# Two more attention groups with an elementwise bonus, a new written order for the first tile, and three down projections in a row at the end

## The chip, the cores and the metric

The kernel runs on one core of a Trainium2 chip. The metric is the device time of one execution in microseconds (us). Three runs of the kernel before took 530.88, 531.82 and 531.77 us; the median is 531.77 us. The core has five engines that run their own instruction queues in order: TensorE (PE in the profile; its weight loads are listed as PEld), VectorE (DVE), ScalarE (ACT), GpSimd (POOL) and SyncE (SP), which here only issues DMAs.

## The reference

The program is a recurrent linear attention whose output goes through a gated feed-forward block.

- Attention, for 4 batches, 8 heads, 768 positions and head size 48: `y[t] = r[t] @ (state + (u*k[t]) v[t]^T)`, then `state = w * state + k[t] v[t]^T`. The term with `u` is the bonus: it weighs the position's own key and value.
- Feed-forward, for the 3072 rows of width 384 that the attention gives: `gate = sigmoid(x @ w_gate)`, `val = x @ w_val` (both 384 to 1536), `out = (gate * val) @ w_out` (1536 to 384). All in float32.

## The kernel before, in words

**Attention.** The 768 positions are cut into 12 chunks of 64, the heads into 2 sets, which gives 24 groups, numbered n = 0 to 23 (`GROUPS`, line 34; chunk n // 2). A group's work is: scores of keys against queries (`scores`, 64 small matmuls on TensorE or 32, see below), a masked copy of the scores into `score` (`keep`, VectorE), outputs from the state of the chunk before (`from_state`, 32 small matmuls, none for chunk 0), outputs from the scores (`apply`, 32), the chunk's contribution to the state (`outer`, 32), the decay of the state (ScalarE) and its sum (VectorE). `x_high` (ScalarE) and `x_low` (VectorE) split the outputs into two float32r parts in `xt`, the input of the feed-forward. `fills` moves rows of `xt` inside SBUF with DMAs.

**The bonus, in two ways** (`FIRST`, line 39). Groups below `FIRST` get it from TensorE: ScalarE scales the keys by u (`bonus_keys`, four instructions), `scores` makes a second set of 32 matmuls of these against the queries, and `keep` copies its diagonal with a second masked copy. `apply` puts a drain of TensorE between the outputs from the state and those from the scores, since the two use the array's quarters differently. Groups from `FIRST` on get it elementwise: the queries in token order are loaded into `dec` (`load_own`), GpSimd multiplies them by the keys and by u (`own_tokens`, two instructions), VectorE sums over the head size and spreads the sums over a diagonal (`diagonal`, two instructions), and ScalarE turns a part of the queries round (`turn_queries`, two copies). The state is laid out differently from `FIRST` on; the two groups before it change it over (`add_state`, lines 435 to 453).

**Feed-forward.** The rows are cut into 6 tiles of 512 columns (two chunks each), the 1536 hidden columns into 12 blocks f. An item is one block of one tile: `up` (18 matmuls of 512 columns, 9 for the gate and 9 for the value, each half into its own bank of a ring of three PSUM banks), `gate` (sigmoid on ScalarE, product on VectorE, `h_high` on ScalarE, `h_low` on GpSimd) and `down` (9 matmuls into three accumulators). `h` has two buffers (pool `hq`). A matmul is split in three float32r products (`PASS`). In the first tile the first two blocks are done in halves of 256 columns, one per chunk, which makes items 0 to 3; items 4 to 13 are blocks 2 to 11 of the first tile.

**Weights.** Each of the 12 blocks (1152 KB) is loaded as 64-bit floats and turned into two float32r parts on the core: `cast_top` (ScalarE), `join_words` (VectorE), `round_weights` (ScalarE), `rest_of_weights` (GpSimd or VectorE).

**Order.** The engines follow the written order (`manual_schedule`); a wait stops all that stands behind it on its engine. `START` (lines 43 to 57) is the order of groups 0 to 7 and items 0 to 13, one step a word: L, X, Y, W load channels (512 KB), tokens (400 KB), own tokens (192 KB) and weights; A are the bonus keys, R/Rv the queries (GpSimd/VectorE), t their turn, k the keys, T/Tv the token keys; Z `scores`, K `keep`, I `apply` with the outputs from the state, O `outer`, d and s (sa on ScalarE) decay and sum of the state, h and l the two parts of x, F `fills`; b and i `own_tokens` and `diagonal`; c, j, w and o/ov the four steps of a block of weights (c0, j0, w0, o0 for halves of block 0); U `up`, g, m, H and q/qv the four steps of the gate (qv: `h_low` on VectorE), D `down`; tc, tk, ti, tp, tr, tt, tn make constants and decay tables. All loads go through SP's queue in this order. Channels and tokens have three buffers each, `dec` two, the ring of banks three: a load waits at the head of SP's queue for a free buffer.

From item 14 on a loop (line 674) writes the order: for each item `up`, at four of twelve items one attention group (from n = 8), `gate`, and then `down` of the item before. After the last item `store_last` scales the accumulators on ScalarE and VectorE in turn and issues four DMAs on SP.

Of the kernel before, what the change touches and what calls it, by code (L numbers as in the profile page):

```python
# [35 lines left out]
TILE_OF = [c // 2 for c in range(NC)]  # L36


HALF, FIRST = 2, 8
SLOTS = (0, 3, 6, 9)  # L40


START = """
L.0 W.0 L.1 X.0 W.1 L.2 X.1 X.2 tc A.0 tk ti.1 R.0 ti.0 k.0 tp tr Z.0 tt K.0 I.0 c0.0 A.1 c0.1 tn
h.0 c.1 T.2 T.1 k.1 Rv.1 j0.1 l.0 Tv.0 j0.0 Z.1 O.0 W.2 F.0 W.3 L.3 L.4 W.4 X.3 j.1 K.1 I.1 O.1 A.2
w0.0 sa.0 w.1 h.1 w0.1 o0.1 o.1 R.3 Rv.2 k.2 o0v.0 l.1 s.1 Z.2 K.2 U.0 I.2 O.2 g.0 c.2 d.2 A.3 m.0
U.1 H.0 g.1 h.2 j.2 k.3 s.2 l.2 q.0 T.3 m.1 F.2 L.5 W.8 X.4 L.6 W.5 W.6 L.7 X.5 F.1 X.6 L.8 W.7 Z.3
K.3 I.3 O.3 w.2 A.4 k.4 H.1 c.3 h.3 l.3 R.4 D.0 Z.4 U.2 d.3 s.3 g.2 c.4 j.3 w.3 j.4 qv.1 m.2 o.2
U.4 H.2 g.4 w.4 A.5 K.4 q.2 U.3 D.2 g.3 Rv.5 m.3 k.5 ov.3 m.4 T.4 I.4 O.4 Z.5 H.3 A.6 d.4 h.4 H.4
c.6 c.5 k.6 s.4 K.5 l.4 Tv.5 j.6 R.6 q.3 D.1 D.3 U.5 I.5 g.5 h.5 j.5 qv.4 l.5 m.5 o.4 Z.6 D.4 R.7  # L50
O.5 U.6 A.7 d.5 H.5 K.6 k.7 s.5 q.5 T.6 w.5 ov.5 U.7 c.8 c.7 g.6 j.7 m.6 L.9 X.8 ub Y.8 W.9 W.10
X.7 I.6 Z.7 O.6 D.5 w.6 g.7 ov.6 d.6 w.7 H.6 s.6 j.8 qv.6 h.6 l.6 m.7 w.8 ov.7 H.7 qv.7 D.6 U.8 K.7
R.8 c.9 ov.8 g.8 m.8 Tv.7 H.8 U.9 qv.8 g.9 k.8 j.9 w.9 o.9 m.9 D.7 U.10 g.10 H.9 c.10 j.10 m.10 q.9
D.8 I.7 H.10 d.7 Z.8 O.7 h.7 w.10 D.9 s.7 U.11 ov.10 l.7 W.11 F.5 X.9 F.6 F.3 F.7 F.4 Y.9 qv.10
g.11 c.11 j.11 D.10 U.12 m.11 w.11 R.9 ov.11 U.13 g.12 H.11 qv.11 m.12 H.12 qv.12 g.13 t.8 D.11 b.8
i.8 D.12 K.8 k.9 m.13 H.13 q.13 b.9 T.9 t.9 i.9 T.8
"""


# [1 line left out]
def rwkv_then_moe(ctx: ExitStack, tc: tile.TileContext, wd, ub, ch, tk, rt, wt, rk0, vn0, wd0, out):  # L61
    nc = tc.nc
# [33 lines left out]
    w = wu[:, 0]  # L96
# [292 lines left out]
    def apply(n):  # L389
        c, g = GROUPS[n]  # L390
        v, t = toks[n][:, 1], score[n % 2]
        if n < FIRST:
            outputs(n)
            if c:
                nc.tensor.drain()
        for p, p2 in PP:
            for s in range(2):
                for gm in range(2):
                    be, row = gm ^ s, slice(64 * gm, 64 * gm + 64)
                    m, at = D if s else 64, (4 * p + 2 * be + p2) * D  # L400
# [101 lines left out]
    class Moe:  # L502
# [34 lines left out]
            c, h = self.cols, self.h[f]  # L537
            eng.tensor_tensor(h[:, 1, c], self.sg.pop(f)[:, c], h[:, 0, c], ALU.subtract)  # L538

        def gate(self, f):  # L540
            self.sigmoid(f)
            self.product(f)
            self.h_high(f)
            self.h_low(f)

        def down(self, f):

# [63 lines left out]
    def finish(i):  # L611
        ti, h, f = items[i]
        moe_of(items[i]).down(f)
        if f == NF - 1:
            if ti == len(TILES) - 1:
                store_last(accs[ti], TILES[ti][0])
            else:
                store(accs[ti], slice(TILES[ti][0], TILES[ti][-1] + 1))
# [274 lines left out]
```

## Time and profile before

| | |
|---|---|
| runs of the kernel before | 530.88, 531.82, 531.77 us; median 531.77 us |
| profiled execution | 534.72 us, of which the span from first to last instruction is 532.9 us |
| TensorE busy | 510.4 us, 96% of the span |
| VectorE, ScalarE, GpSimd busy | 203.4, 186.9, 189.9 us |
| DMA from memory and back | 47.84 MB, on SP's queue |

The profile is of one execution, slower than the median of the others. Busy TensorE time is modelled: a matmul's bar lasts longer than the distance to the next, so the distance between weight loads (PEld) says more about the pace than the bars do. A line of the timeline merges instructions of one kind: start, time from the first start to the last end, engine, source line, operation, names and shapes, count, and in brackets the idle time before it and what ended that.

### The profile page before, as it was taken

The numbers are of one execution on the slowest core, as the hardware profiler recorded it, in microseconds if no ns is written. First come the engines' busy times: TensorE is split into PE (matmuls) and PEld (weight loads), VectorE is DVE, ScalarE is ACT, GpSimd is POOL, SyncE is SP. The second block draws the span as 40 slices with busy tenths as digits, with TensorE's granted clock in tenths as the row PEclk, the third lists the DMA queues.
The fourth block names the chain that finished last, engine by engine and source line by source line (L and its number), as shares of the span: only waits on it lengthen the run. The fifth ranks groups of instructions, "written<-read, shape, count | busy, mean of one in ns | idle before, by whom it ended". The sixth has DMA issues, their size and how long they took to land. (4 is left out here: it accounts for less than half of the span.)

```text
span 532.9 us, 11951 instructions
## 1 busy us (share of the span) xinstructions
PE 510.4 (96%) x5204; PEld 424.4 (80%) x5204; DVE 203.4 (38%) x344; ACT 186.9 (35%) x396; POOL 189.9 (36%) x159
## 2 busy tenths in 40 slices
PE   3689999999999999999999999999999999999994
PEld 3678878888888888888888888888888888888883
DVE  8857868464243242341431532431442211111111
ACT  5577665545133233233232331331432222212111
POOL 4362530406453352443452552542253111112210
PEclk9999999999999999999999999999999999999999
DMA  8939736030321230420221420312400000100001
GB/s 321 366 111 352 301 112 284 4 103 21 127 87 26 71 106 1 145 86 17 80 61 48 145 87 0 97 34 72 146 17 2 11 11 10 60 0 1 0 2 64
DMA packets 15723, 47.84 MB, mean 90 GB/s; under 512 B 2384, under 2 KB 5200, under 8 KB 14256
## 3 DMA queue, kind: packets, MB, share of 16 engines
q1 hardware_dynamic: 15664, 47.01, 25.3%
q8 instruction: 43, 0.70, 0.6%
q14 instruction: 16, 0.13, 0.1%
HBM read 39.92 MB, written 4.72 MB: 84 GB/s over the span
## 5 line engine op out<-in xcount | busy, mean ns | idle before, releaser
L516 PE MATMUL ring<-xt,wx 128*128 128x512 f32 (+1 forms) x1332 | 309.9, 387 | 0.9 <-ACT sg L525 0.5
L516 PEld LDWEIGHTS ring<-xt,wx 128*128 128x128 f32 x1332 | 247.8, 191 | 51.3 <-ACT sg L525 0.7
L538 POOL TENSOR_TENSOR h<-sg,h 128x512 fp32r<-128x512 f32 (+1 forms) x66 | 88.5, 1340 | 259.5 <-ACT h L534 259.5
L554 PE MATMUL acc<-h,wx 128*128 128x512 f32 (+1 forms) x666 | 161.6, 388 | 0.4 <-POOLq L714 0.4
L554 PEld LDWEIGHTS acc<-h,wx 128*128 128x128 f32 x666 | 121.2, 188 | 25.6 <-POOLq L714 0.8
L529 DVE TENSOR_TENSOR sg<-ring,sg 128x512 f32<-128x512 f32 (+1 forms) x74 | 50.0, 676 | 237.0 <-PE ring L516 235.6
L525 ACT ACTIVATE sg<-ring 128x512 f32<-128x512 f32 (+1 forms) x74 | 43.4, 586 | 157.4 <-PE ring L516 157.4
L534 ACT CAST h<-sg 128x512 fp32r<-128x512 f32 (+1 forms) x74 | 45.0, 608 | 144.2 <-DVE sg L529 138.2
L293 POOL TENSOR_TENSOR dec<-chan,tabk 128x512 f32<-128x512 f32 x21 | 29.0, 1381 | 12.5 <-PE ring L337 12.4
L478 DVE TENSOR_TENSOR xt<-ring,xt 112x256 fp32r<-112x256 f32 (+1 forms) x52 | 19.9, 418 | 33.1 <-ACT xt L474 33.0
L308 POOL TENSOR_TENSOR toks<-toks,tabn 128x384 f32<-128x384 f32 x19 | 24.0, 1267 | 13.7 <-DMA toks<-in_tk 13.7
L314 POOL TENSOR_TENSOR dec<-dec,toks 128x384 f32<-128x384 f32 x16 | 16.3, 1020 | 27.3 <-DMA dec<-in_rt 27.3
L304 DVE TENSOR_TENSOR chan<-chan,tabk 128x512 f32<-128x512 f32 x24 | 25.0, 1042 | 0.9 <-ACT dec L287 0.9
L375 PE MATMUL sc<-dec,chan 48*64 48x64 f32 x768 | 17.4, 231 | 7.7 <-DVE chan L304 7.6
L383 DVE COPY_PREDICATED score<-masks,sc 128x512 f32<-128x512 int32 x32 | 23.9, 747 | 1.9 <-PE sc L375 1.1
L428 ACT ACTIVATE state<-state,pw 112x96 f32<-112x96 f32 x80 | 23.4, 362 | 2.6 <-PE ring L337 2.6
L337 PE MATMUL ring<-score,toks 64*48 64x64 f32 (+1 forms) x768 | 17.2, 230 | 5.0 <-DVE score L383 4.1
L447 DVE TENSOR_TENSOR state<-state,ring 48x192 f32<-48x192 f32 (+1 forms) x52 | 17.9, 350 | 9.7 <-ACT xt L474 4.7
L375 PEld LDWEIGHTS sc<-dec,chan 48*64 48x64 f32 x768 | 15.0, 145 | 8.1 <-POOL dec L293 7.6
L247 DVE SCALAR_TENSOR_TENSOR wf<-wr,top 128x1152 int32<-128x1152 int32 (+1 forms) x13 | 16.9, 1310 | 9.4 <-ACT top L240 5.7
L337 PEld LDWEIGHTS ring<-score,toks 64*48 64x48 f32 (+1 forms) x768 | 14.6, 137 | 6.4 <-DVE score L383 4.8
L474 ACT CAST xt<-ring 112x256 fp32r<-112x256 f32 (+1 forms) x52 | 16.7, 364 | 7.6 <-PE ring L337 7.3
(60 smaller groups left out, 250.5 us busy)
## 6 DMA issues: line engine op xcount, KB each, us to landing
wr<-in_wt SPq DMA_DIRECT2D x11, 1152.0 KB, 9.2
chan<-in_ch SPq DMA_DIRECT2D x24, 512.0 KB, 4.2
toks<-in_tk SPq DMA_DIRECT2D x24, 400.0 KB, 4.8
out_y<-wf SPq DMA_DIRECT2D x17, 256.0 KB, 2.5
dec<-in_rt SPq DMA_DIRECT2D x16, 192.0 KB, 2.7
xt<-xt SPq DMA_DIRECT2D x30, 64.0 KB, 2.3
wr<-in_wt SPq DMA_DIRECT2D x2, 576.0 KB, 5.4
xt<-xt SPq DMA_DIRECT2D x12, 32.0 KB, 4.2
```

The source lines that it names most:

```text
L293: eng.tensor_tensor(v4(t[:, 0]), v4(chan[n][:, 0]), bc2(table_of(n)[:, :, ::-1]), ALU.mult)
L304: nc.vector.tensor_tensor(v4(k), v4(k), bc2(table_of(n)), ALU.mult)
L308: eng.tensor_tensor(v4(k), v4(k), bc2(tabn[:, 4 * g : 4 * g + 4]), ALU.mult)
L337: nc.tensor.matmul(yb[n][bank][64 * half : 64 * half + m, cs], lhsT, rhs, start=first, stop=stop, skip_group_check=True,)
L375: nc.tensor.matmul(sc[64 * gm : 64 * gm + 64, be, o : o + C], kk[row, cs : cs + C], rr[row, cs : cs + C], start=True, stop=True,)
L383: nc.vector.copy_predicated(t.rearrange("q (b m i) -> q b m i", b=2, m=4), masks[:, m].bitcast(I32).unsqueeze(1).unsqueeze(1).broadcast_to ...
L516: nc.tensor.matmul(o[:, self.cols], w[a][:, g * DM + kt * P : g * DM + (kt + 1) * P], self.x[:, kt, b, self.cols], start=(k == 0), stop=(k ...
L525: nc.scalar.activation(sg[:, c], self.pair[f][0][:, c], AF.Sigmoid, scale=UP)
L529: nc.vector.tensor_tensor(sg[:, c], self.pair.pop(f)[1][:, c], sg[:, c], ALU.mult)
L534: nc.scalar.copy(out=h[:, 0, c], in_=sg[:, c])
L538: eng.tensor_tensor(h[:, 1, c], self.sg.pop(f)[:, c], h[:, 0, c], ALU.subtract)
L554: nc.tensor.matmul(self.acc[d][:, self.cols], w[a][:, 2 * DM + d * P : 2 * DM + (d + 1) * P], h[:, b, self.cols], start=(f == 0 and k == 0 ...
```

## The change

- `FIRST` goes from 8 to 6 and a new `LATE` = 8 marks where the loop takes over: groups 6 and 7 get the bonus elementwise, while `apply` still opens its banks itself for all groups of `START`.
- `START` is written anew: an order of the same first 8 groups and 14 items, with the steps that the elementwise bonus of groups 6 and 7 needs.
- At the end, `down` of the third and second last items is written after `up` and `gate` of the last, so that three `down` follow one another, and `h_low` of the last item goes to VectorE.
- In `store_last` the DMA of the accumulator half that ScalarE scales is issued on ScalarE's queue.

```diff
--- before.py
+++ after.py
@@ -36,24 +36,24 @@
 TILE_OF = [c // 2 for c in range(NC)]
 
 
-HALF, FIRST = 2, 8
+HALF, FIRST, LATE = 2, 6, 8
 SLOTS = (0, 3, 6, 9)
 
 
 START = """
-L.0 W.0 L.1 X.0 W.1 L.2 X.1 X.2 tc A.0 tk ti.1 R.0 ti.0 k.0 tp tr Z.0 tt K.0 I.0 c0.0 A.1 c0.1 tn
-h.0 c.1 T.2 T.1 k.1 Rv.1 j0.1 l.0 Tv.0 j0.0 Z.1 O.0 W.2 F.0 W.3 L.3 L.4 W.4 X.3 j.1 K.1 I.1 O.1 A.2
-w0.0 sa.0 w.1 h.1 w0.1 o0.1 o.1 R.3 Rv.2 k.2 o0v.0 l.1 s.1 Z.2 K.2 U.0 I.2 O.2 g.0 c.2 d.2 A.3 m.0
-U.1 H.0 g.1 h.2 j.2 k.3 s.2 l.2 q.0 T.3 m.1 F.2 L.5 W.8 X.4 L.6 W.5 W.6 L.7 X.5 F.1 X.6 L.8 W.7 Z.3
-K.3 I.3 O.3 w.2 A.4 k.4 H.1 c.3 h.3 l.3 R.4 D.0 Z.4 U.2 d.3 s.3 g.2 c.4 j.3 w.3 j.4 qv.1 m.2 o.2
-U.4 H.2 g.4 w.4 A.5 K.4 q.2 U.3 D.2 g.3 Rv.5 m.3 k.5 ov.3 m.4 T.4 I.4 O.4 Z.5 H.3 A.6 d.4 h.4 H.4
-c.6 c.5 k.6 s.4 K.5 l.4 Tv.5 j.6 R.6 q.3 D.1 D.3 U.5 I.5 g.5 h.5 j.5 qv.4 l.5 m.5 o.4 Z.6 D.4 R.7
-O.5 U.6 A.7 d.5 H.5 K.6 k.7 s.5 q.5 T.6 w.5 ov.5 U.7 c.8 c.7 g.6 j.7 m.6 L.9 X.8 ub Y.8 W.9 W.10
-X.7 I.6 Z.7 O.6 D.5 w.6 g.7 ov.6 d.6 w.7 H.6 s.6 j.8 qv.6 h.6 l.6 m.7 w.8 ov.7 H.7 qv.7 D.6 U.8 K.7
-R.8 c.9 ov.8 g.8 m.8 Tv.7 H.8 U.9 qv.8 g.9 k.8 j.9 w.9 o.9 m.9 D.7 U.10 g.10 H.9 c.10 j.10 m.10 q.9
-D.8 I.7 H.10 d.7 Z.8 O.7 h.7 w.10 D.9 s.7 U.11 ov.10 l.7 W.11 F.5 X.9 F.6 F.3 F.7 F.4 Y.9 qv.10
-g.11 c.11 j.11 D.10 U.12 m.11 w.11 R.9 ov.11 U.13 g.12 H.11 qv.11 m.12 H.12 qv.12 g.13 t.8 D.11 b.8
-i.8 D.12 K.8 k.9 m.13 H.13 q.13 b.9 T.9 t.9 i.9 T.8
+L.0 L.1 X.2 L.2 X.0 W.0 F.4 X.1 W.6 X.4 L.3 tc tk ti.1 R.2 A.0 A.2 tp tr k.0 Rv.0 tt tn ti.0 Tv.2
+Tv.0 Z.0 K.0 I.0 O.0 A.1 c0.1 k.2 j0.1 Tv.1 s.0 c0.0 w0.1 h.0 c.6 l.0 Z.2 K.2 I.2 j0.0 k.1 h.2 l.2
+d.2 L.4 X.3 F.0 W.10 F.2 o0.1 R.1 R.3 A.3 Z.1 O.2 K.1 s.2 I.1 O.1 w0.0 sa.1 h.1 T.3 k.3 j.6 Z.3 K.3
+I.3 O.3 A.4 w.6 T.4 R.4 o0.0 d.3 l.1 o.6 k.4 s.3 h.3 l.3 Z.4 L.6 W.8 W.5 W.3 X.5 W.2 F.3 L.5 W.11
+X.9 W.9 F.5 X.6 Y.6 ub F.1 W.1 W.7 W.4 L.7 U.0 U.2 g.0 c.10 m.0 H.0 j.10 g.2 m.2 H.2 K.4 q.2 U.8
+w.10 ov.10 qv.0 c.8 g.8 c.5 Rv.6 m.8 j.8 D.0 U.12 D.2 H.8 g.12 w.8 j.5 t.6 c.3 I.4 d.4 w.5 m.12 k.6
+q.8 o.5 ov.8 Z.6 O.4 D.8 h.4 H.12 s.4 l.4 q.12 j.3 U.10 g.10 c.2 j.2 m.10 U.7 H.10 g.7 w.2 w.3 m.7
+ov.3 c.9 A.5 D.12 q.10 j.9 H.7 b.6 D.10 U.5 w.9 g.5 ov.2 qv.7 D.7 U.4 c.1 k.5 m.5 H.5 c.7 q.5 g.4
+j.1 i.6 ov.9 j.7 Tv.6 k.7 Rv.5 K.6 m.4 D.5 I.6 O.6 Z.5 w.7 d.6 h.6 w.1 l.6 Rv.7 s.6 L.8 L.9 F.6 X.7
+X.8 Y.7 Y.8 U.11 o.7 K.5 Tv.5 I.5 Z.7 O.5 H.4 g.11 q.4 c.4 j.4 m.11 D.4 U.9 d.5 R.8 h.5 t.8 ov.1
+l.5 s.5 b.7 U.3 w.4 H.11 g.9 m.9 qv.11 g.3 t.7 c.11 H.9 i.7 ov.4 T.7 b.8 K.7 m.3 qv.9 j.11 k.8 U.1
+D.11 g.1 H.3 U.6 q.3 g.6 w.11 o.11 m.6 i.8 H.6 D.9 Z.8 I.7 O.7 q.6 D.6 d.7 m.1 s.7 Y.9 U.13 H.1 h.7
+l.7 F.7 q.1 D.1 D.3 b.9 R.9 g.13 t.9 k.9 m.13 H.13 K.8 qv.13 Tv.8 Tv.9 i.9
 """
 
 
@@ -389,9 +389,9 @@
     def apply(n):
         c, g = GROUPS[n]
         v, t = toks[n][:, 1], score[n % 2]
-        if n < FIRST:
+        if n < LATE:
             outputs(n)
-            if c:
+            if c and n < FIRST:
                 nc.tensor.drain()
         for p, p2 in PP:
             for s in range(2):
@@ -537,11 +537,11 @@
             c, h = self.cols, self.h[f]
             eng.tensor_tensor(h[:, 1, c], self.sg.pop(f)[:, c], h[:, 0, c], ALU.subtract)
 
-        def gate(self, f):
+        def gate(self, f, eng=nc.gpsimd):
             self.sigmoid(f)
             self.product(f)
             self.h_high(f)
-            self.h_low(f)
+            self.h_low(f, eng)
 
         def down(self, f):
 
@@ -586,10 +586,11 @@
             nc.sync.dma_start(
                 out=out[d * P : (d + 1) * P, c : c + 2], in_=o.rearrange("q (c t) -> q c t", t=CT)
             )
+        queues = nc.scalar, nc.sync
         for i in range(2):
             o = hp.tile([P, 512], F32, name="sg")[:, 0:CT]
             out_of(engines[i], o, acc[2][:, i * CT : (i + 1) * CT])
-            nc.sync.dma_start(out=out[2 * P : 3 * P, c + i], in_=o)
+            queues[i].dma_start(out=out[2 * P : 3 * P, c + i], in_=o)
 
 
     halves = [(0, g) for g in range(HALF)] + [(1, g) for g in range(HALF)] + [(2, g) for g in range(HALF, NF)]
@@ -669,7 +670,7 @@
             late.append(n)
 
     late = []
-    n = FIRST
+    n, last = LATE, len(items) - 1
     load(n + 2)
     for i in range(n0, len(items)):
         ti, h, f = items[i]
@@ -684,7 +685,7 @@
             apply(n)
             if goes_on:
                 outer(n)
-        m.gate(f)
+        m.gate(f, nc.vector if i >= last else nc.gpsimd)
         if late:
             diagonal(late.pop())
         if goes_on:
@@ -696,7 +697,8 @@
                 add_state(n)
             if n + 1 < len(GROUPS):
                 keep(n + 1)
-        finish(i - 1)
+        for j in {last - 1: (), last: (last - 2, last - 1)}.get(i, (i - 1,)):
+            finish(j)
         if attend:
             prepare(n + 2)
             fills(n)
@@ -705,7 +707,7 @@
         if i == n0 + 8:
             range_flag()
     assert n == len(GROUPS)
-    finish(len(items) - 1)
+    finish(last)
 
 
     order.close()
```

## Rows read from the trace of the kernel before

**Rows 1.** Busy time by window: stretch, us, five engines' busy time, clock, DMA, GB/s.
```profile
0.00:41.38 41.38, 26.91 (x690) 24.25 (x690) 30.68 (x55) 24.83 (x57) 19.57 (x26) 1.00 0.70 262
41.38:121.59 80.21, 79.02 (x938) 65.99 (x933) 54.69 (x76) 47.85 (x87) 22.57 (x15) 1.00 0.50 190
121.59:521.36 399.77, 399.77 (x3567) 330.86 (x3566) 116.26 (x211) 112.64 (x250) 146.46 (x118) 1.00 0.17 52
```

**Rows 2.** Timeline of TensorE's weight loads, the first 50 us.
```profile
7.60 0.97 PEld L375 LDWEIGHTS sc<-dec,chan 48*64 48x64 f32 x32 [7.60 <-POOL dec L293]
8.41 1.02 PEld L375 LDWEIGHTS sc<-chan,dec 48*64 48x64 f32 x32
...
24.18 3.49 PEld L516 LDWEIGHTS ring<-xt,wx 128*128 128x128 f32 x16 [0.48 <-DVE xt L478]
27.89 0.93 PEld L337 LDWEIGHTS ring<-dec,state 48*64 48x64 f32 x32 [0.22 <-issue]
29.27 0.96 PEld L337 LDWEIGHTS ring<-score,toks 64*64 64x64 f32 x32 [0.45 <-issue]
...
31.18 1.99 PEld L516 LDWEIGHTS ring<-xt,wx 128*128 128x128 f32 x9
33.89 1.13 PEld L516 LDWEIGHTS ring<-xt,wx 128*128 128x128 f32 x9 [0.72 <-ACT sg L525]
...
41.38 8.68 PEld L516 LDWEIGHTS ring<-xt,wx 128*128 128x128 f32 x54
```

**Rows 3.** Timeline of weight loads, 82 to 127 us.
```profile
82.25 8.13 PEld L516 LDWEIGHTS ring<-xt,wx 128*128 128x128 f32 x36
...
98.89 0.54 PEld L337 LDWEIGHTS ring<-dec,state 48*64 48x64 f32 x32 [0.35 <-issue]
99.74 0.55 PEld L337 LDWEIGHTS ring<-score,toks 64*64 64x64 f32 x32 [0.31 <-issue]
100.19 0.57 PEld L375 LDWEIGHTS sc<-dec,chan 48*64 48x64 f32 x32
...
125.98 0.14 PEld L337 LDWEIGHTS ring<-dec,state 48*64 48x64 f32 x2 [0.35 <-issue]
...
126.43 0.57 PEld L375 LDWEIGHTS sc<-dec,chan 48*64 48x64 f32 x32
```

**Rows 4.** Timeline of ScalarE, 5 to 15 us.
```profile
9.33 1.28 ACT L287 ACTIVATE dec<-chan,wu 128x128 f32<-128x128 f32 x4 [1.77 <-DMA chan<-in_ch]
...
11.21 0.45 ACT L202 COPY tabn<-acc 128x384 f32<-128x384 f32 x1
```

**Rows 5.** Groups by line and shape, 0 to 125 us: count, busy us, mean ns, idle before.
```profile
L383 DVE COPY_PREDICATED score<-masks,sc 128x512 f32<-128x512 int32 x17 | 12.6, 744 | 1.4 <-PE sc L375 1.1
L324 DVE TENSOR_TENSOR score<-masks,bonus 128x512 f32<-128x512 f32 x2 | 1.6, 798 | 0.1
L308 DVE TENSOR_TENSOR toks<-toks,tabn 128x384 f32<-128x384 f32 x3 | 1.6, 550 | 2.2 <-DMA toks<-in_tk 2.2
L319 DVE TENSOR_REDUCE bonus<-dec 128x8 f32<-128x384 f32 x2 | 1.1, 549 | 5.0 <-POOL dec L315 5.0
...
L314 POOL TENSOR_TENSOR dec<-dec,toks 128x384 f32<-128x384 f32 x2 | 2.0, 1020 | 0.0
```

**Rows 6.** Timeline of the last 12 us.
```profile
521.36 2.45 PEld L554 LDWEIGHTS acc<-h,wx 128*128 128x128 f32 x11
...
523.27 1.29 POOL L538 TENSOR_TENSOR h<-sg,h 128x512 fp32r<-128x512 f32 x1 [4.83 <-ACT h L534]
524.61 1.46 PEld L554 LDWEIGHTS acc<-h,wx 128*128 128x128 f32 x7 [0.80 <-POOLq L714]
...
527.49 0.88 SPq L592 DMA_DIRECT2D out_y<-sg  x2
```

**Rows 7.** DMA issues: names, queue, operation, count, size, median us to landing.
```profile
chan<-in_ch SPq DMA_DIRECT2D x24, 512.0 KB, 4.2
...
out_y<-sg SPq DMA_DIRECT2D x2, 128.0 KB, 2.7
```

## The prediction

> **What bounds the kernel now.** I read the busy time by window first. TensorE is busy in all of the 399.77 us from 121.59, where item 14 starts, to 521.36 us; from 41.38 to 121.59 it misses 1.2 of 80.2 us; ahead of 41.38 it is busy for 26.9 us only [rows 1]. The middle loop is written the same before and after, so two stretches can change: the first tile up to item 14, and the end. I then read the weight loads for TensorE's pace. A full `up` takes 8.13 / 2 = 4.07 us and a `down` half of that [rows 3]; U.2, U.4 and U.3 together took 8.68 us, so a half `up` takes 2.3 [rows 2]. Early on the pace is half: 16 loads of 256 columns took 3.49 us at 24.18 (218 ns each) and nine took 1.99 at 31.18, but nine took 1.13 (126 ns) at 33.89, and 32 small loads took 0.81 us at 8.41 - 7.60 against 0.45 at 100.19 - 99.74 [rows 2, 3]. The granted clock reads 1.00 in all three windows [rows 1], so the level of 1.2 GHz is read from the spacing: the pace doubled between 33.2 and 33.9, after TensorE had worked from 27.89 on with pauses under 1 us.
>
> **The elementwise bonus of groups 6 and 7.** Each group loses 32 matmuls of scores (0.45 us), and its outputs from the state no longer drain: they took 0.85 us with a drain (98.89 to 99.74) and 0.45 without (125.98 to 126.43) [rows 3]. That is 2 x (0.45 + 0.4) = 1.7 us of TensorE, all on the path, since TensorE is full there. VectorE loses a masked copy (0.74) and gains `diagonal` (0.55 + 0.80); ScalarE swaps the four bonus keys (1.28) for two copies; GpSimd gains two multiplications of 1.02 a group, in place of nothing; SP gains two loads of own tokens [rows 4, 5]. VectorE is busy for 54.7 of 80.2 us here, ScalarE 47.9, GpSimd 22.6 [rows 1]: they hide it, 0 on the path. Without that cover it would cost up to 2 x (0.6 + 2.0) = 5.2 us.
>
> **The new first tile: when U.0 starts.** The old order starts U.0 at about 23 us, at half pace, and mixes it with the attention. The new one does groups 0 to 3 and the scores of group 4 first; then TensorE has feed-forward work without end. So the time at which U.0 starts decides. I follow the chain in the new order. The second channel load landed at 9.33 with 2176 KB queued up to its end [rows 4]; now L.2 has 1936 KB up to its end, which makes between 9.33 x 1936 / 2176 = 8.3 and 9.33; I take 8.7. A.2, which waits for it, stands in front of tn on ScalarE: 8.7 + 1.28 + 0.45 = 10.4 [rows 4]. Tv.2 and Tv.0 (0.55 each) 11.5, K.0 (two copies of 0.74) 13.0 [rows 5]. I.0, O.0 and Z.2 at half pace (0.95, 0.95, 2 x 0.81 and 0.4 to the next engine [rows 2]) 17.0, K.2 18.5, j0.0 and k.1 (0.7 each, as VectorE's other operations of that size [rows 5]) 19.9, Z.1 22.0, K.1 23.5, s.2 (0.7) 24.2, I.1 and O.1 26.1, Z.3 28.2, K.3 29.7. Then l.1 stands on VectorE ahead of the bank that I.3 needs: half of its four pieces of 256 columns (0.4 each, half of a 512-column operation) 30.5. I.3 with its drain 1.4 (27.89 to 29.27) + 0.95 [rows 2], O.3 0.95, Z.4 1.65: U.0 starts at 35.5.
>
> The loads keep ahead of this. X.4 waits at the head of SP's queue for a token buffer, which O.0 frees at 15; behind it L.3, with 4.2 us from issue to landing [rows 7], is there at 20, before A.3 can run (21.5, behind d.2). X.3 waits for O.2 (22.7); behind it stand F.0, W.10, F.2 and then weight blocks in a row. TensorE uses a block of 1152 KB in 6.1 us, which needs 193 GB/s; the first window moved 262 with the DMA engines busy for 0.70 of it [rows 1].
>
> **From U.0 to item 14.** Old: 41.38 to 121.59, 80.2 us, of which 1.2 idle [rows 1]. The new stretch has U.0, U.1 and D.0 besides (2 x 2.3 + 1.13 = 5.7) and lacks the 1.7 above: 84.2, less the old idle time 83.0. Two costs come on top. The pace at U.0: between 0 (already full, as after 5.5 us of work with short pauses; from 30.5 on it is that) and 4.6 us (U.0 and U.2 wholly at half pace); I take 1.1, half of U.0, as the nearer row is the rise at 33.9. New stalls: between 0 and 3. The closest places of the written order are D.0 and F.7. While U.8 runs (4.07) VectorE has m.2, K.4, ov.10 and qv.0 ahead of D.0, half of 0.8, 1.5, about 1.8 for 1152 columns at the 1.56 ns of 798 / 512 and 0.4, together 4.1 [rows 5]. After I.7 TensorE has O.7, D.6, U.13, D.1 and D.3, 8.8 us, while s.7 and l.7 (2.6), four DMA issues (0.44 each [rows 6]) and a landing (2.7 [rows 7]) take 7.1 until U.14 may read. I take 1.0, about the old 1.2. Sum: 35.5 + 83.0 + 1.1 + 1.0 = 120.6 instead of 121.59: **-1.0**. The start of U.0 lies between 33.5 (if the 0.2 us that I add at most steps for the way from engine to engine are too many) and 38 (rival 2).
>
> **The end.** Before, `down` of the last item has its first two matmuls at once and waits for `h_low` on GpSimd (1.29): the loads stop for 0.80 us [rows 6]. Now two more `down` (4.0 us) lie between. The last `h` takes the buffer that the third last `down` reads, so `h_high` can start only when that ends, 2.2 us after the last `up`; with a cast of 0.6 (0.45 for 384 columns [rows 4]) and `h_low` on VectorE, 0.8 as its product of that size [rows 5], it is ready at 3.7, and the two `down` end at 4.0: hidden (with 1.29 for each, GpSimd's time, it would be 4.8, and 0.3 us would be lost at the third matmul), **-0.8** (bounds 0 and -0.8). The last two DMAs took 0.88 us on SP one behind the other [rows 6]; one goes to ScalarE's queue, which is idle then, so the last is issued **0.4** earlier. No row shows a DMA issued from ScalarE: bounds -0.45, and +1.5 if it lands as slowly as the channel loads, 4.2 us against 2.7 for these stores [rows 7]; I take -0.4, by the like DMA on SP.
>
> Sum: -1.0 - 0.8 - 0.4 = -2.2 us. The profiled execution took 534.72 us, 532.9 of span and 1.8 around it: it becomes 532.5. It lay 2.95 above the median of the runs, so the median goes from 531.77 to 529.6.
>
> **The rivals.**
> (1) *The first tile runs with no new stalls and at full pace from U.0*: 2.1 us better, 527.5. For it: TensorE works almost without pause from 30.5. Against: old stalls of 1.2 in a like order.
> (2) *U.0 comes late, so only the end gains*: if the token buffer of X.4 came free with O.2 (22.7) and not with O.0 (15), L.3 would land at 26.5 (between the 2.7 and 4.2 us of [rows 7] after its issue), A.3 would run then and not at 21.5, and Z.3, two steps behind it, start at 28.5 and not 26.1: U.0 2.4 us later, -1.0 + 2.4 - 1.2 = +0.2, or 532.0. Against: any of the three buffers should do, and O.0 comes first. The same price has contention of VectorE and GpSimd along the chain.
> (3) *Half pace lasts* (slower): the front part is now 28 us of small matmuls with pauses for VectorE, and the full-size work starts only at U.0. If the pace stays at half for as long as it did after the first full-size matmuls of before (24.18 to 33.17, 9.0 us), 4.5 us are lost in place of 1.1: -2.2 + 3.4 = +1.2, 533.0. It decides from 8.7 us of half pace on. For it: at 24.18 TensorE ran 3.49 us with no pause and stayed at half [rows 2]; against: full pace came soon after the dense stretch from 27.89. The Trainium skill's page "TensorE: Matmul & The Clock Gate" (Part 1: The HAM clock gate) says that the throttled clock is the default and that activity releases it. By that rule putting the sparse attention in front gives TensorE a cold start into the feed-forward; the half pace up to 33 us in this trace agrees, though its clock column does not show it.
>
> **How the numbers follow.** Runs of this kernel differ by 0.2%, 1.06 us, which is what counts as no change. Forecast 0.50, with its own range 528.5 to 530.7; rival 1 0.17; rival 2 0.18; rival 3 0.15. Faster: forecast and rival 1, 0.67; same: rival 2, 0.18; slower: rival 3, 0.15. The range goes from a little below rival 1 (526.9) to rival 3 (533.0).
>
> **What would show it.** U.0 (the first 128-column loads with `xt`) at 35.5 and full pace within 2 to 4 us of it; item 14 at 120.6; VectorE's copies at 11.5, 17, 22 and 28; 32 instead of 64 scores matmuls in groups 6 and 7; no stop among the last 27 weight loads; last DMA issued some 1.9 us after the last weight load ends and not 2.3 (528.37 - 526.07 [rows 6]). The prediction is wrong if U.0 comes after 38, if the half pace goes on through U.8, if TensorE idles over 3 us between U.0 and item 14, or if the span ends more than the old 6.8 us after the last weight load (532.9 - 526.07).

## The result and the profile after

The change makes the kernel slower: 535.15 us (median of 6 runs, 534.54 to 537.07) against 531.80 us (6 runs, 529.54 to 532.58), a ratio of 1.0073 with a 95% interval of 1.0049 to 1.0097. The forecast was 529.6. The profiled execution took 534.54 us with a span of 532.8; forecast 532.5 us.

By window (stretch, us, busy time of PE, PEld, DVE, ACT, POOL, clock, DMA), cut where U.0 and item 14 start and where the last weight load ends, as in [rows 1]:
```profile
0.00:37.04 37.04, 19.27 (x644) 17.51 (x644) 27.78 (x54) 20.39 (x51) 17.56 (x25) 0.82 0.71 252
37.04:121.49 84.45, 83.87 (x917) 71.67 (x914) 59.59 (x78) 51.36 (x87) 33.94 (x23) 0.98 0.52 193
121.49:525.78 404.29, 404.02 (x3585) 334.15 (x3584) 118.19 (x217) 114.77 (x254) 141.69 (x113) 1.00 0.17 54
```
U.0 starts at 37.04 (forecast 35.5), item 14 at 121.49 (forecast 120.6; 121.59 in [rows 1]). The stretch between, 84.45 us with 0.58 idle, is what was forecast (85.1). The weight loads up to U.0, where [rows 2] has those of before:
```profile
8.57 0.94 PEld L375 LDWEIGHTS sc<-dec,chan 48*64 48x64 f32 x32 [0.55 <-DVE dec L293]
13.20 0.96 PEld L337 LDWEIGHTS ring<-score,toks 64*64 64x64 f32 x32 [2.83 <-issue]
16.57 0.74 PEld L337 LDWEIGHTS ring<-dec,state 48*64 48x64 f32 x25
18.10 0.19 PEld L337 LDWEIGHTS ring<-dec,state 48*64 48x64 f32 x7 [0.79 <-issue]
18.65 0.57 PEld L337 LDWEIGHTS ring<-score,toks 64*64 64x64 f32 x32 [0.36 <-DVE score L383]
...
20.40 0.93 PEld L375 LDWEIGHTS sc<-chan,dec 48*64 48x64 f32 x32
21.14 0.84 PEld L337 LDWEIGHTS ring<-toks 64*64 64x64 f32 x23
23.53 0.32 PEld L337 LDWEIGHTS ring<-toks 64*48 64x48 f32 x9 [1.56 <-issue]
...
30.63 0.92 PEld L337 LDWEIGHTS ring<-dec,state 48*64 48x64 f32 x30 [2.58 <-issue]
...
33.49 0.78 PEld L375 LDWEIGHTS sc<-dec,chan 48*64 48x64 f32 x18
36.20 0.25 PEld L375 LDWEIGHTS sc<-dec,chan 48*64 48x64 f32 x10 [1.92 <-issue]
```
Three sets of 32 are cut in the middle by a stop that no other engine ends ("issue" names a wait whose cause the profile doesn't show): I.2's outputs from the state after 25 loads (0.79 us), O.2 after 23 (1.56), Z.4 after 20 (1.92; two of the 20 stand in a line that is left out). By the names, the rest of a set reads the same tiles as its beginning, so a late operand is unlikely; the runs below test it. (The 2.83 at 13.20 and the 2.58 at 30.63 bear the same name but fit a wait for VectorE: K.0 ends at 13.14, and the first half of l.1, by half of its 1.72 us, at 30.54.) The pace changes too: 32 loads in 0.57 at 18.65, 0.93 at 20.40. The granted clock is 0.50, the level of 1.2 GHz, from 20.50 to 34.20, and again for part of U.0, U.2 and U.8, whose 54 loads from 37.04 on took 9.74 us; two halves and a full `up` took 8.68 before [rows 2]:
```profile
20.50:34.20 13.70, 9.41 (x319) 0.50 0.49 158
34.20:37.20 3.00, 1.22 (x52) 1.00 0.76 224
37.20:41.00 3.80, 3.80 (x20) 0.55 0.99 390
41.00:60.00 19.00, 18.82 (x218) 1.00 0.99 399
```
The end, in answer to [rows 6]: 27 loads in a row without a stop, and one DMA issue on each of two queues.
```profile
519.70 6.08 PEld L554 LDWEIGHTS acc<-h,wx 128*128 128x128 f32 x27
525.50 1.11 SPq L586 DMA_DIRECT2D out_y<-wf  x2
526.71 0.38 ACTq L593 DMA_DIRECT2D out_y<-sg  x1
527.16 0.33 SPq L593 DMA_DIRECT2D out_y<-sg  x1
```
The last issue ends 1.71 us after the last load (525.78; forecast 1.9), but the span ends 7.0 us after it, not earlier than the 6.8 of before; of the prediction's own signs of being wrong this is the only one that came. In the loop D.15 stops 0.69 us until 141.96: its `h_low` stands on GpSimd behind the products of group 10, for whose own tokens GpSimd sat idle 7.19 us until 137.13. The trace of before has no stop there (nine loads in 2.00 us from 140.13).

### The profile page after: what moved, and what is told of

The parts are those of the page before. It is cut to its first block, busy times and chain, and to the rows that moved or that the text cites. A ratio compares the mean times of both kernels' runs of the same rounds, so it can differ in the third digit from the quotient of the medians.

```text
span 532.8 us, 11836 instructions
## 1 busy us (share of the span) xinstructions
PE 507.6 (95%) x5140; PEld 423.3 (79%) x5140; DVE 206.5 (39%) x350; ACT 186.9 (35%) x392; POOL 193.2 (36%) x161
## 4 chain that ended last, share of the span: by engine, by line
PE 80%; DVE 2%; POOL 1%; DMA 1%; ACT 0%; issue 0%; SPq 0%; DVEq 0%; ACTq 0%; POOLq 0%
PE ring L516 48%; PE acc L554 25%; PE ring L337 5%; PE sc L375 2%; DMA dec<-in_rt 1%; POOL h L538 0%; DVE score L383 0%; DVE chan L304 0%; ACT state L428 0%; DVE wf L247 0%; POOL dec L314 0%; POOL dec L315 0%; DVE state L447 0%; POOL toks L308 0%; DVE wf L567 0%
## 5 line engine op out<-in xcount | busy, mean ns | idle before, releaser
L538 POOL TENSOR_TENSOR h<-sg,h 128x512 fp32r<-128x512 f32 (+1 forms) x68 | 92.4, 1359 | 261.5 <-ACT h L534 261.5
L478 DVE TENSOR_TENSOR xt<-ring,xt 112x256 fp32r<-112x256 f32 (+1 forms) x52 | 20.0, 419 | 34.1 <-ACT xt L474 33.8
L314 POOL TENSOR_TENSOR dec<-dec,toks 128x384 f32<-128x384 f32 x18 | 19.5, 1086 | 30.0 <-DMA dec<-in_rt 29.9
L293 POOL TENSOR_TENSOR dec<-chan,tabk 128x512 f32<-128x512 f32 x20 | 26.3, 1316 | 9.0 <-DMA chan<-in_ch 6.7
L304 DVE TENSOR_TENSOR chan<-chan,tabk 128x512 f32<-128x512 f32 x24 | 23.1, 963 | 0.1
L337 PEld LDWEIGHTS ring<-dec,state 48*64 48x64 f32 (+1 forms) x416 | 13.1, 141 | 9.8 <-issue 9.4
L375 PE MATMUL sc<-dec,chan 48*64 48x64 f32 x768 | 18.3, 233 | 2.5 <-issue 1.8
L315 POOL TENSOR_TENSOR dec<-dec,utab 128x384 f32<-128x384 f32 x18 | 20.1, 1115 | 1.4
L258 POOL TENSOR_TENSOR wx<-wf,wx 128x1152 fp32r<-128x1152 f32 (+1 forms) x6 | 14.1, 2362 | 17.3 <-ACT wx L255 17.3
L308 POOL TENSOR_TENSOR toks<-toks,tabn 128x384 f32<-128x384 f32 x15 | 17.9, 1195 | 5.6 <-DMA toks<-in_tk 5.6
L300 ACT COPY chan<-dec 64x256 f32<-64x256 f32 x36 | 14.6, 406 | 13.5 <-POOL dec L293 13.1
```

What stands on the lines that cost most here:

```text
L293: eng.tensor_tensor(v4(t[:, 0]), v4(chan[n][:, 0]), bc2(table_of(n)[:, :, ::-1]), ALU.mult)
L304: nc.vector.tensor_tensor(v4(k), v4(k), bc2(table_of(n)), ALU.mult)
L337: nc.tensor.matmul(yb[n][bank][64 * half : 64 * half + m, cs], lhsT, rhs, start=first, stop=stop, skip_group_check=True,)
L375: nc.tensor.matmul(sc[64 * gm : 64 * gm + 64, be, o : o + C], kk[row, cs : cs + C], rr[row, cs : cs + C], start=True, stop=True,)
```

## Experiments

Each ratio is to the kernel before, timed beside it, with its 95% interval; gains "by the ratios" are differences of two such ratios. The name in brackets is that of the run. `N.k` is a step that writes k small float32 matmuls of the identity into a free accumulator, with 8 columns where nothing else is said; each makes two pairs of weight load and matmul, and nothing reads them. In the diffs of the written order "..." stands for steps that are left out.

**Before again** (`before_again`). No edit.

> The kernel before, unchanged. Theory P: the execution profiled first (span 532.9 us) was a long one, because TensorE kept to half pace until 33 us in it; its runs have a median of 531.8 and so spans near 530.0. A second profile should then have item 14 near 118.7 us instead of 121.59, with full pace (32 small loads in 0.45 us) well before 33 us, and the same 6.12 us an item later. Rival: the long one is long in the middle or at the end, and item 14 stands at 121 to 122 again. The ratio to itself should be 1.000 within 0.003.

531.91 us, ratio 1.0001 [0.9978, 1.0023]. Its profiled execution shows how far those of one kernel differ at the front:
```profile
28.10 0.55 PEld L337 LDWEIGHTS ring<-dec,state 48*64 48x64 f32 x32 [0.22 <-issue]
...
35.99 0.55 PEld L337 LDWEIGHTS ring<-score,toks 64*64 64x64 f32 x32 [1.31 <-DVE score L383]
```
The same set of I.3 in the trace of the prediction:
```profile
37.96 0.55 PEld L337 LDWEIGHTS ring<-score,toks 64*64 64x64 f32 x32 [1.32 <-DVE score L383]
```
The first set at full pace stands at 28.10, where [rows 2] had the half pace to 33; I.3's sums start at 35.99 (37.96) and item 14 at 119.85 (121.59). The five further profiles with the old order at the front (below) have full pace by 23.3 to 28.5 and I.3 at 34.6 to 36.1. The execution that the prediction was worked out from was 1.9 to 3.3 us late there. Theory P is right in half: item 14 came earlier, but not at 118.7, and this execution was a long one too (534.50 us), because its end took longer: 23.3 us from the start of item 72 to the end of the span, against 21.75.

**The end alone** (`tail_only`: old order; the lines that matter).
```diff
-        m.gate(f)
+        m.gate(f, nc.vector if i >= last else nc.gpsimd)
...
-        finish(i - 1)
+        for j in {last - 1: (), last: (last - 2, last - 1)}.get(i, (i - 1,)):
+            finish(j)
...
-            nc.sync.dma_start(out=out[2 * P : 3 * P, c + i], in_=o)
+            queues[i].dma_start(out=out[2 * P : 3 * P, c + i], in_=o)
```


> The kernel before with the end of the changed kernel (three down in a row, h_low of the last item on VectorE, one DMA on ScalarE's queue), old first tile. By the prediction's term: 1.2 us faster, ratio 0.9977. By the trace of the changed kernel: the stop of 0.80 us is gone, but the last stores land no earlier, so 0.6 to 0.8 us faster, ratio 0.9987. If it is slower than before, the second queue costs more than its issue time saves.

530.22 us, ratio 0.9962 [0.9941, 0.9984]: -2.0 us. The interval, -0.9 to -3.1, holds the 1.2 of the prediction.

**The order and the bonus without the end** (`order_only`: the changed kernel without the lines above).

> The changed kernel with the old end: new order of the first tile and elementwise bonus for groups 6 and 7. Theory: the whole loss sits here, 3.3 us and the 0.7 that the end gives, so 4.0 us slower than before, ratio 1.0075. Rival: the loss sits in the end or is a matter of the profiled execution, ratio 1.000 to 1.002.

536.73 us, ratio 1.0098 [1.0069, 1.0128]: +5.2. Its stops: 1.57 in I.2 after 25 loads, 0.85 in O.2 after 23, 2.52 in Z.4 after 20. The same places, other lengths. The loss sits in this part of the change, as the theory has it.

**40 pairs more ahead of the attention** (`shift20`, on the changed kernel).
```diff
-L.3 tc tk ti.1
+L.3 tc N.20 tk ti.1
```


> The changed kernel with 20 small matmuls (32 x 8 outputs, unused) written ahead of TensorE's first step, in the 7 us in which it waits anyway; each float32 matmul is two loads and two matmuls in the trace, so 40 load and matmul pairs more. In the changed kernel TensorE stops in the middle of three sets of small matmuls with no data to wait for: after 221, 347 and 602 pairs from its start, 126 and 255 apart. Theory C (the instructions themselves come in pieces of 256, that is some 128 pairs, and run dry): the stops move 40 pairs up in the order, to the second half of Z.2 (49th of 64 pairs), Z.1 (47th of 64) and O.3 (14th of 32). Theory D (a wait for data or a semaphore that the profile doesn't name): the stops stay in the outputs of group 2 from the state (25th), in O.2 (23rd) and in Z.4 (18th to 22nd). Time: within 1.5 us of the changed kernel by either.

532.86 us, ratio 1.0017 [0.9995, 1.0038]: with 40 pairs more to do the kernel is 3.0 us faster than the changed one (1.0073) by the ratios, 2.3 by the medians. The cut sets are whole:
```profile
16.68 1.08 PEld L337 LDWEIGHTS ring<-dec,state 48*64 48x64 f32 x32
...
21.71 1.02 PEld L337 LDWEIGHTS ring<-toks 64*64 64x64 f32 x32
...
30.00 0.92 PEld L337 LDWEIGHTS ring<-dec,state 48*64 48x64 f32 x30 [2.58 <-issue]
...
34.15 0.97 PEld L375 LDWEIGHTS sc<-dec,chan 48*64 48x64 f32 x32 [1.08 <-POOL wx L258]
...
36.10 9.76 PEld L516 LDWEIGHTS ring<-xt,wx 128*128 128x128 f32 x54
```
The written order and its operands are the same, so the stops were not for data. Neither theory foretold this: the sets that theory C named (Z.2, Z.1, O.3) are whole too, and the gain is above the 1.5 us that both allowed. The half pace at U.0 is still there (9.76), so the 3.0 us are not the pace. Between the two traces the difference is smaller than between the ratios: U.0 at 36.10 against 37.04, item 14 at 120.75 against 121.49, and a span of 531.5 against 532.8.

**128 pairs more** (`shift64`, on the changed kernel).
```diff
-L.3 tc tk ti.1
+L.3 tc N.50 tk ti.1
-Z.0 K.0 I.0
+Z.0 K.0 N.14 I.0
```


> The changed kernel with 128 small pairs of weight load and matmul added on TensorE that nothing reads: 100 at 1.4 us and 28 between the scores and the first sums of group 0; shift20 had 40. Theory (TensorE's instructions arrive in pieces of 256, that is 128 pairs of load and matmul, so that adding a whole piece puts the seams back where they were in the changed kernel): TensorE stops inside I.2, O.2 or Z.4 again, after about 25, 23 and 18 of their loads, for 0.7 to 1.9 us with no release from another engine, and the time is that of the changed kernel or above it by what the added pairs delay group 0: 535 to 536.5. Rival (any added work at the head spreads the stream, so that the stops go, whatever the number): the sets are whole as in shift20, 532.9 to 533.9.

535.46 us, ratio 1.0063 [1.0033, 1.0093]: the loss is back, and so are two of the three cuts at their places, O.2 (0.28) and Z.4 (2.61); that in I.2 is not.
```profile
22.10 0.83 PEld L337 LDWEIGHTS ring<-toks 64*64 64x64 f32 x23
23.21 0.31 PEld L337 LDWEIGHTS ring<-toks 64*48 64x48 f32 x9 [0.28 <-issue]
...
33.11 0.75 PEld L375 LDWEIGHTS sc<-dec,chan 48*64 48x64 f32 x20 [0.25 <-issue]
36.47 0.40 PEld L375 LDWEIGHTS sc<-dec,chan 48*64 48x64 f32 x10 [2.61 <-issue]
```
So the stops go by the number of instructions, not by the step. Counted from the first weight load, those of the changed kernel stand behind 221, 347 and 600 loads, the two of shift64 behind 475 and 728, which is 128 more than the last two. Other traces below agree: bonus_on_tensor stops behind 221, 347, 474 and 600 loads, tail_only, in the old order, behind 222, 347, 472 and 599 (0.83, 0.20, 1.31 and 0.17 us), and warm_new, with 40 pairs more, 1.67 us behind 347, which is now another place of Z.1. The page of the changed kernel shows what has that size: a DMA queue of the kind "instruction" moves 0.69 MB in 42 pieces, 16 KB each, for 10,280 matmuls and loads, about 245 a piece.
```profile
q8 instruction: 42, 0.69, 0.5%
```
One such piece moves in each of the stretches around the three stops, 15.0 to 18.3, 20.5 to 23.9 and 32.5 to 37.0 us:
```profile
q8 instruction: 1, 0.02, 2.1%
q8 instruction: 1, 0.02, 2.0%
q8 instruction: 1, 0.02, 1.7%
```
These pieces begin at 15.8, 21.2 and 33.6 us, and the stops end 2.3, 2.4 and 2.6 us later. In the seven traces that stop behind such counts, a stop ends 2.2 to 3.0 us after the start of a piece. In shift20 the pieces begin at 12.9, 18.4, 22.1 and 26.4, and TensorE passes the four counts at 16.2, 21.2, 25.7 and 32.4, in each case 2.8 us or more after the piece began: it doesn't stop. So TensorE waited for its own instructions at the seams, and a seam costs time only where its piece begins late. The Trainium skill ("Runtime: NRT & Kernel Launch", Instruction fetch mechanics) names blocks of 16 KB, or 256 instructions. The traces agree: 126 and 253 pairs lie between the stops of the changed kernel. The same section of the Trainium skill calls the cost of crossing such a boundary mostly hidden. Here it is not: it cost 0.2 to 2.6 us a stop in sets of small matmuls.

**Full-size work in the waits, new order** (`warm_new`): as shift20, with 20 of the 40 pairs 128 columns wide (`M`; the expectation says 24) and the others 32.
```diff
-L.3 tc tk ti.1
+L.3 tc N.10 M.6 tk ti.1
-Z.0 K.0 I.0
+Z.0 K.0 M.4 I.0
```


> The changed kernel with 40 pairs of weight load and matmul added on TensorE that nothing reads, as in shift20, but 24 of them with 128 columns: 32 pairs at 1.4 us, ahead of the transposes of the token table, and 8 between the scores and the first sums of group 0, in a wait. Theory (what is left of the loss is TensorE's half pace up to 37 us, which the new order keeps and the old one leaves at 23 to 34 us): the sets of 32 weight loads take 0.57 us from about 15 us on, U.0, U.2 and U.8 take 8.7 us for 54 loads instead of 9.76, item 14 at or before 119, the median 530.0 to 531.0, against 532.86 of shift20. Rival A (the pace is hidden behind VectorE's and the DMAs' chain; the order itself is longer): item 14 at 120.5 to 121, median 532.5 to 533.5. Rival B (the added work falls into the pace's windows but the pace drops again in the waits between 16 and 34 us): half pace again at U.0, median 532.5 to 533.

533.14 us, ratio 1.0022 [1.0004, 1.0039]. By the trace it is rival B: the pace rises and is lost again behind a stop at a seam. The time lies in the range of rival A.
```profile
14.29 0.56 PEld L375 LDWEIGHTS sc<-dec,chan 48*64 48x64 f32 x29
...
21.57 0.60 PEld L375 LDWEIGHTS sc<-chan,dec 48*64 48x64 f32 x17 [1.67 <-issue]
21.95 0.98 PEld L337 LDWEIGHTS ring<-toks 64*64 64x64 f32 x32
...
36.33 8.97 PEld L516 LDWEIGHTS ring<-xt,wx 128*128 128x128 f32 x54
```
U.0 is no earlier (36.33; 36.10 in shift20) for the full pace from 14 to 20 us. It is at half pace for a part only (8.97 us), and item 14 comes at 120.17.

**The same in the old order** (`warm_old`, on tail_only).
```diff
-X.2 tc A.0
+X.2 tc M.7 N.3 A.0
-Z.1 O.0 W.2
+Z.1 O.0 M.3 W.2
```


> tail_only (old order, new end) with 26 such pairs on TensorE, 20 of them with 128 columns: 20 at 1.4 us and 6 after the first state of group 0. Theory (the old order's spread of 529.6 to 534.5 us is the moment at which the pace rises, 23 to 34 us): full pace before 18 us in every execution, item 14 at 117 to 118, median 529.0 to 529.8 and a narrower spread than tail_only's 528.64 to 531.23. Rival (the spread comes from the DMAs): median 530.2 and the same spread.

530.84 us, ratio 0.9985 [0.9969, 1.0001], spread 530.2 to 532.65. The theory failed: in the trace full pace came at 27.8, not before 18, and nothing was gained.

**The end with one queue** (`tail_one_queue`: tail_only, all four DMAs on SP).

> tail_only without the ScalarE queue: both last outputs are issued by SP, as before the change. Theory (the two terms of the end are alike in size: the stop 0.8 and the rest from the second queue): median 530.8 to 531.2, half way between 530.22 and 531.9, and the last two issues take 0.9 to 1.4 us on SP instead of 0.33. Rival A (the queue is worth nothing, the stop is worth more than it lasted): 530.2. Rival B (the queue is worth all): 531.9.

530.60 us, ratio 0.9980 [0.9959, 1.0001], between the theory and rival A. The interval overlaps that of tail_only: the second queue is worth 0.4 us by the medians, 1.0 by the ratios, and not settled. From the start of item 72 to the end of the span it took 21.2 us, tail_only 21.1; with the old end 21.75 in the trace of the prediction, 23.3 in before_again and 22.9 in order_only.

**The bonus of groups 6 and 7 back on TensorE** (`bonus_on_tensor`, on the changed kernel). A.7 stands behind k.7 here, so group 7's bonus is taken from keys that are already scaled; the work is the same.
```diff
-HALF, FIRST, LATE = 2, 6, 8
+HALF, FIRST, LATE = 2, 8, 8
-X.6 Y.6 ub ... j.5 t.6 c.3 ... H.7 b.6 D.10 ... j.1 i.6 ov.9
+X.6 ub ... j.5 A.6 c.3 ... H.7 D.10 ... j.1 ov.9
-s.6 L.8 L.9 ... X.8 Y.7 Y.8 ... s.5 b.7 U.3 ... g.3 t.7 c.11 ... H.9 i.7 ov.4
+s.6 L.8 A.7 L.9 ... X.8 Y.8 ... s.5 U.3 ... g.3 c.11 ... H.9 ov.4
```


> The changed kernel with the bonus of groups 6 and 7 back on TensorE (FIRST and LATE 8: two further steps of scaled keys on ScalarE in place of loads of own tokens, products on GpSimd, sums and turned queries), all else as changed. Theory (the elementwise bonus takes 1.7 us off TensorE, as the prediction put it): 536.9, item 14 at 123.2. Rival A (the pairs fall into waits or the elementwise work costs as much elsewhere): 535.2, item 14 at 121.5. Rival B (the elementwise bonus costs more than it saves): under 534.5.

537.29 us, ratio 1.0097 [1.0069, 1.0126]: 1.3 us over the changed kernel by the ratios, 2.1 by the medians; the intervals overlap, so the times alone don't settle it. The stretch from the end of U.8 to item 14, which holds groups 6 and 7, shows it in the traces, this run first, then the changed kernel:
```profile
48.16:124.93 76.77, 75.36 (x925) 63.84 (x924) 51.52 (x68) 45.96 (x84) 28.64 (x18) 1.00 0.40 147
46.82:121.49 74.67, 74.09 (x861) 62.57 (x860) 54.40 (x72) 45.63 (x80) 33.19 (x22) 1.00 0.46 165
```
64 matmuls fewer, and 2.1 us less. In this order the bonus edit gains about what was predicted.

**The bonus and the end in the old order** (`old_bonus_tail`, with the changed kernel's lines of `FIRST` and `LATE`).
```diff
-Z.5 H.3 A.6 d.4 ... j.6 R.6 q.3 ... o.4 Z.6 ... O.5 U.6 A.7 d.5 H.5 K.6 k.7 s.5 q.5 T.6
+Z.5 H.3 ub Y.6 d.4 ... j.6 R.6 t.6 q.3 ... o.4 b.6 Z.6 ... O.5 U.6 X.7 Y.7 d.5 H.5 i.6 K.6 k.7 t.7 s.5 q.5 T.6 b.7
-ub Y.8 W.9 W.10 X.7 ... U.8 K.7
+Y.8 W.9 W.10 ... U.8 i.7 K.7
```


> The order of before with two of the three parts of the change: the new end, and the bonus of groups 6 and 7 elementwise (their two steps of scaled keys on ScalarE become loads of own tokens, products on GpSimd, sums and turned queries; X.7 is issued seven steps earlier). Theory (the loss is the new order alone; from 70 to 118 us TensorE runs without a wait of over 0.4 us in the old order too, so 128 pairs fewer are 1.7 us): 528.5. Rival A (the pairs fall into waits): 530.2, as tail_only. Rival B (GpSimd's products and VectorE's sums for two groups more hold up the rounded weights and the gates in the old order): 531 to 532.

535.54 us, ratio 1.0074 [1.0044, 1.0103]; the theory failed by 7 us (the two groups have 64 pairs fewer, not 128). Group 6's own tokens were issued at 53.86 and landed at 63.0, with the DMA engines busy for 0.96 of that time; GpSimd waited for the load, VectorE for GpSimd, TensorE for VectorE's state behind it:
```profile
63.03 1.00 POOL L314 TENSOR_TENSOR dec<-dec,toks 128x384 f32<-128x384 f32 x1 [8.00 <-DMA dec<-in_rt]
...
65.17 0.55 DVE L319 TENSOR_REDUCE bonus<-dec 128x8 f32<-128x384 f32 x1 [3.13 <-POOL dec L315]
...
68.91 0.47 PEld L516 LDWEIGHTS ring<-xt,wx 128*128 128x128 f32 x2 [3.48 <-DVE state L447]
```

**The same, with the waiting steps moved back** (`old_bonus_tail2`).
```diff
-o.4 b.6 Z.6 ... H.5 i.6 K.6 k.7 t.7 s.5 q.5 T.6 b.7 w.5 ov.5 U.7 c.8 c.7 g.6 j.7 m.6
+o.4 Z.6 ... H.5 s.5 q.5 b.6 w.5 ov.5 T.6 U.7 c.8 c.7 g.6 j.7 i.6 K.6 m.6 k.7 t.7 b.7
```


> old_bonus_tail with the same work but the steps that wait for group 6's own tokens (they landed at 63.0 us) moved behind what TensorE needs first: on VectorE the state of group 5, the rounded rest of weights 5 and the joined words of weights 7 go ahead of group 6's sums and score; on GpSimd the gate of item 5 goes ahead of group 6's products. Theory (the 3.5 us that TensorE stood at 65.4 to 68.9 us in old_bonus_tail was VectorE queued behind the load of own tokens, and the elementwise bonus itself is worth 1.7 us): that stand falls under 0.5 us, item 14 at 116 to 117.5, median 528.3 to 529. Rival A (GpSimd and VectorE have no room for two more groups between 60 and 75 us; another wait takes its place): 530 to 533. Rival B (the queued load is not the reason): 535.5 again.

532.63 us, ratio 1.0021 [0.9998, 1.0044]: 2.8 us back by the ratios, and still above tail_only. Rival A: the stand of 3.48 is gone, two of 1.02 (rest of weights 5) and 1.22 (a product of the gate behind group 6's score) take its place.

**An earlier U.0** (`early_up`, on shift20).
```diff
-T.3 k.3 j.6 Z.3 K.3 I.3 O.3 A.4 w.6 T.4 R.4 o0.0 d.3 l.1 o.6 k.4 s.3 h.3 l.3 Z.4
+T.3 k.3 l.1 Z.3 K.3 I.3 O.3 A.4 R.4 T.4 o0.0 d.3 k.4 s.3 h.3 l.3 j.6 w.6 o.6 Z.4
```


> shift20 with four steps moved: the low parts of group 1's outputs go ahead of group 3's score on VectorE, the joined words of weights 6 behind group 4's keys, and on GpSimd group 4's queries go ahead of its token keys and the rest of weights 6 behind the first half of weights 0 and group 4's work; nothing is added or left out. In shift20 group 3's sums stood 2.58 us until 30.0, and group 4's keys took 3.12 us of VectorE (0.68 for group 3's) while GpSimd took 4.00 us over the rests of weights. Theory (the first up projection starts late by VectorE's and GpSimd's queues, and what it starts earlier the first tile ends earlier, as the prediction's sum has it): the stand at 30.0 goes, U.0 at 34.0 to 34.8 instead of 36.10, item 14 at 118.6 to 119.3 instead of 120.75, median 531.0 to 531.5 against 532.86. Rival A (half the gain is eaten later, by weights 6 that come late for U.8 or by tokens): U.0 early but item 14 at 120 or later, median 532.0 to 532.9. Rival B (something else holds U.0): U.0 at 36, 532.9.

532.52 us, ratio 1.0002 [0.9985, 1.0019]. U.0 came at 34.12, 1.98 us earlier than in shift20, as the theory has it. Weights 6 were late for U.8, by 1.20 us, as rival A has it, and item 14 came 1.34 us earlier, at 119.41, between the two. The gain of 0.8 us by the ratios is within the intervals.
```profile
34.12 4.23 PEld L516 LDWEIGHTS ring<-xt,wx 128*128 128x128 f32 x27
...
40.89 3.96 PEld L516 LDWEIGHTS ring<-xt,wx 128*128 128x128 f32 x18 [1.20 <-POOL wx L258]
```
No version timed here is below the end alone, tail_only, which is faster than both kernels.

## Why the prediction was wrong

**The step that failed: "It lay 2.95 above the median of the runs, so the median goes from 531.77 to 529.6."** It took the excess of the profiled execution as something that a change leaves alone. The excess sat in the very stretch that is written anew: that execution had the half pace up to 33 us and was 1.9 to 3.3 us late at I.3, which no other profile of the old order was. (An old execution can be long elsewhere: before_again lost 1.5 us at the end.) In the new order U.0 comes at 36.1 to 37.9 us, the pace still half there, in the changed kernel and in order_only, bonus_on_tensor, shift20, shift64 and, for a part, warm_new: none of these six traces shows a better front to fall back on. After, the median lies 0.6 above the profiled execution instead of 2.95 below: 3.6 of the 5.6 us between forecast and result. What a typical execution of the old order has in hand is seen at 36 us (stretch, us, PE busy and count, clock, DMA): tail_only first, then the changed kernel, then the trace of the prediction.
```profile
0.00:36.00 36.00, 21.29 (x601) 1.00 0.78 295
36.00:118.42 82.42, 81.32 (x1023) 1.00 0.51 187
```
```profile
0.00:36.00 36.00, 18.43 (x599) 0.81 0.71 254
36.00:121.49 85.49, 84.72 (x958) 0.98 0.52 193
```
```profile
0.00:36.00 36.00, 22.72 (x512) 1.00 0.76 290
36.00:121.59 85.59, 83.21 (x1125) 1.00 0.49 182
```
By 36 us tail_only has done as many matmuls as the changed kernel, but two half `up` are among them (4.6 us); the new order has these before it and only 1.7 us less of bonus, which makes 2.9 us more, and 85.5 against 82.4 us are left to go. The trace of the prediction was 89 matmuls behind, and hid this.

The other steps:

- *U.0 at 35.5*: 37.04, and item 14 0.9 us late, the largest part of the other 2.0 us. The chain itself was right within 1 us (K.0 ended at 13.1, forecast 13.0; Z.1 began at 19.9, as forecast; K.1 ended at 23.1, forecast 23.5; K.3 at 29.8, forecast 29.7; Z.4 began at 33.4, forecast 33.8). Z.4 then took 3.6 us instead of 1.65, 1.92 of it the stop at the instruction seam, a cost that the sum had no term for. shift20 and shift64 size all that hangs on the seams at 3.0 and 2.5 us by their ratios, shift20's trace at 1.3. The old order can stop at seams too (0.83 us in I.1 and 1.31 in Z.3 in tail_only); in the trace of the prediction these sets are whole, so it gave no row for the cost.
- *Half pace 1.1, new stalls 1.0*: 1.06 (9.74 - 8.68) and 0.58: right.
- *Bonus -1.7*: right here (1.3 to 2.1). That VectorE and GpSimd hide it holds for this order; in the old one they did not, and old_bonus_tail lost 6.0 us to tail_only by the ratios. That this is near the 5.2 for "without that cover" is chance: what was lost there is largely the wait for a load.
- *The end -1.2*: the stop is gone (14.24 us from item 72 to the last load, 14.92 before), but against the profiled execution of before it gave 0.5, by the ratio of tail_only 2.0. From item 72 on the old end took 21.75 us in the trace of the prediction, 23.3 and 22.9 in the other two, so that trace had a short one; the new end took 21.3 in the changed kernel. SP's two pairs of issues took 1.62 and 0.88 us in the trace of the prediction, 2.01 and 1.39 in before_again, 2.34 and 0.89 in order_only; why they differ was not tried. No run settles the 0.4 of the second queue.
- *No change within 1.06 us*: that came from three runs. In one set of 17 the runs of the kernel before spread from 528.23 to 534.45 us.
- *The loop*: 0.5 us longer, by D.15's stop, not foreseen; in shift20 it is absent.

Rival 3 had the right sign, at 0.15, but its condition did not come: the half pace cost 1.06 us from U.0 on, not 4.5. It priced the half pace against a trace that had it too; that the price lies in what other executions of before do without it is argued. warm_new had the full pace from 14 to 20 us and gained nothing by it, and warm_old's rise came no earlier than that of other old executions (27.8). Rival 2's late channels did not come either: Z.3 began at 26.0 (forecast 26.1).

What stays open: order_only lies 5.2 us above before although its bonus gains 1.3 to 2.1, so the order costs 6.5 to 7.3. The seams explain 2.5 to 3.0 by the ratios. The rest may be the feed-forward that starts late, of which early_up got back 0.8, not beyond the uncertainty; no run shows it. What full pace from 20 us on would give was not shown, since no run held it.

## What to carry to other kernels

Before a forecast is moved from one profiled execution to the median, ask in which stretch that execution lost its time; if it is the stretch that changes, the difference belongs to the old kernel alone and goes out of the sum. An order that puts many sets of small matmuls in a row can stop at the seams of the instruction stream; in this kernel 40 idle pairs that shift them were worth more than the reordering. Work taken off TensorE that needs a load of its own is only as good as that load's place in the queue.

## What the hardware showed unexpectedly

- TensorE can stop at seams some 128 pairs apart, 0.2 to 2.6 us, when sets of 32 small matmuls follow one another; the stop ends 2.2 to 3.0 us after a 16 KB piece of instructions begins to move. 40 added pairs made the kernel 3.0 us faster by the ratios, 128 added pairs did not (1.0063 against 1.0073).
- The clock column can read 1.00 where the spacing shows half pace: in shift20 1.00 over 20.5 to 34.2 us with sets of 32 loads in 0.94 to 1.02, in the changed kernel 0.50 over the same stretch with 0.93 to 0.96. The trace of shift20 records no change of clock before 39.5 us.
- VectorE's keys of group 4 took 3.12 us in shift20 while GpSimd ran 4.00 us of rests of weights, 0.68 for group 3 beside an idle GpSimd. Beside the same work of GpSimd they took 1.63 in the changed kernel, so the cost is not fixed.
